# A token-mixer kernel: three small affine terms moved into weights, biases and spare rows, and a changed instruction order

## The chip, the cores and the metric

The kernel runs on one core of one Trainium2 chip. The metric is the device time of one execution in microseconds (us), measured on the chip. Executions of one kernel differ by about 1 to 2% (410.51 to 417.81 us in the first four of the kernel before), so every ratio below compares fast executions of two kernels taken in the same rounds, and differences under about 2 us are not read as effects. On one core there is no second die to compare with, so an execution counts as "slow" only where it is more than 1.5% above the fastest of its kernel. The record marks three executions of the kernel before so.

Engine names: PE is TensorE (matmuls), PEld its weight loads, DVE is VectorE, ACT is ScalarE, POOL is GpSimd, SP is the queue that issues most DMAs.

## The reference, cut to what matters

```python
# attention: 8 batches, 8 heads, 576 positions, 64 dims per head
kv  = einsum('bhsd,bhse->bhde', k, v)
out = einsum('bhsd,bhde->bhse', q, kv)
x   = out / sqrt(mean(out*out, -1) + 1e-6) * g_norm        # then heads side by side: (8, 576, 512)

# residual MLP: token mix, then channel mix
a1  = alpha1 * x + beta1
tok = einsum('ts,bsd->btd', w_tok, a1)                     # 576 x 576
u   = x + lam * tok
a2  = alpha2 * u + beta2
ch  = maximum(a2 @ w_ch1, 0) @ w_ch2                       # 512 -> 2048 -> 512
return u + lam * ch
```

Inputs and outputs are fp32. The kernel does the large products in bf16, and those of q, k and v at a higher precision: either in the fp32r type, or with a value split in two bf16 parts.

The affine terms beta1, alpha2 and beta2 can be moved without changing the result. With `d` for the channel and `t` for the token:

- beta1 contributes `rowsum(w_tok)[t] * (lam*beta1)[d]` to `u`. That is an outer product, so it can be extra K rows (rows that the matmul sums over) of the token-mix matmul.
- `a2 @ w_ch1 = u @ (diag(alpha2) w_ch1) + beta2 @ w_ch1`. The first factor is a scaled weight, the second a bias per hidden unit, which a ReLU instruction can add.

## The kernel before

The program is a list of operations with their dependencies, and a list scheduler in Python puts them in order on each engine before the kernel is built. Each operation has an estimated cost, one or several engines that may do it, and a priority; `hasten` gives everything that the first channel matmuls need the highest priority. So a change of any operation or of its estimated cost can change the order of all others.

"Channel 1" means the product with w_ch1 and the ReLU, "channel 2" the product with w_ch2. Batches are taken in pairs: an even batch has 512 columns, the odd one takes the 64 + 64 remaining tokens of both and has 640. The order is software-pipelined: while batch b is in its channel products, batch b+1 is normalised and token-mixed, and batch b+2 has its k, v and q prepared.

The parts that the argument touches:

```python
        def qkv_groups(b):
            def group(cs, hs):
                ...                                                   # q.kv on PE, mean square on ACT and DVE
                P.op("DVE", dve_us(64 * m), lambda e: e.tensor_tensor(                            # L621
                    out=x3, in0=raw(True), in1=inv(), op=ALU.mult), ...)
                P.op(dve_pool(64 * m) if b == 0 else "DVE", dve_us(64 * m),                       # L625
                     lambda e: e.tensor_tensor(out=r_, in0=x, in1=eb, op=ALU.mult), ...)
                P.op("POOL", pool_us(64 * m), lambda e: e.tensor_tensor(                          # L627
                    out=x3, in0=x3, in1=gb, op=ALU.mult), r=xk + ["g"], w=xk, pri=-50)
                if hs.stop == NH:
                    for c in cs:
                        ...
                        P.op("DVE", dve_us(560), lambda e, xa=xa, wc=wc:                          # L634
                             e.scalar_tensor_tensor(
                            out=xa, in0=e2_bc[rows, :], scalar=wsum[rows, wc:wc + 1], in1=xa,
                            op0=ALU.mult, op1=ALU.add), ...)
        ...
        def tok_out(b, c, t):
            ...
            P.op("DVE", dve_us(512), lambda e: e.tensor_tensor(                                   # L655
                out=x, in0=t.flat(rows), in1=x, op=ALU.add), r=[t] + xk, w=xk, pri=-100)
            if b == 0 and c < 4:
                return
            either = {"DVE": dve_us(512), "POOL": pool_us(512)} if b == 0 else "POOL"
            P.op(either, pool_us(512), lambda e: e.tensor_tensor(                                 # L660
                out=a1f[rows, af, :], in0=x, in1=a2_bc[rows, :], op=ALU.mult),
                r=xk + ["a2"], w=[("a1f", af)])
            P.op(either, pool_us(512), lambda e: e.tensor_tensor(                                 # L663
                out=a2b[rows, c, :], in0=a1f[rows, af, :], in1=b2_bc[rows, :],
                op=ALU.add), r=[("a1f", af), "b2"],
                w=[("a2b", c) if c < 4 else ("a2bt", b % 2)])
        ...
        def ut_groups(b):
            def group(c):
                keys = [("a2b", c)] if c < 4 else [("a2bt", 0), ("a2bt", 1)]
                if b > 1:                                             # else by PE
                    P.op("SP", 1.3, lambda e: e.dma_start_transpose(
                        a2t[:, :, 128 * c:128 * c + 128], a2b[:, c, :]), ...)
        ...
            def relu(t, src, dst, key, n):
                P.op("ACT", act_us(n), lambda e: e.activation(dst, src(), ACT.Relu),              # L769
                     r=[t], w=key)
        ...
        def load_w(i):
            if i < 4:
                ...                                                   # w_ch1, by DMA, to stg
                for dj in range(4):
                    P.op({"ACT": act_us(512), "POOL": 0.15 + 512 * 0.0016}, 0,
                         lambda e, dj=dj: copy(
                        e, w1[:, dj, 512 * i:512 * i + 512], stg[:, i % 3, dj]), ...)
            else:
                ...                                                   # w_ch2, by DMA, to stg
                for hh in range(4):
                    P.op(dve_pool(512), 0, lambda e, hh=hh: e.tensor_tensor(                      # L1046
                        out=w2[:, 4 * n + hh, :], in0=stg[:, i % 3, hh], in1=lam_bc[:],
                        op=ALU.mult), ...)
```

Cuts are marked with `...`; the line numbers were added and are those of the profile. `eb` is lam\*alpha1\*g_norm, `e2_bc` lam\*beta1, `wsum` the row sums of w_tok. Not shown: q of every batch is split in two bf16 parts (a cast, L415, and a subtraction, L473), and both are transposed to `qt`, by PE for the first batches and by DMA for the others. In the profile `a2b` is a block of a2 in bf16, `a2t` its transpose (what channel 1 reads), `ht` the output of the ReLU, `kr` and `vr` the rounded k and v, `qs` the split q, and `ps` a tile in PSUM.

## Time and profile before

Median of three executions: 412.77 us (410.51 to 416.17). The profiled execution, a fourth, took 417.36 us and has a span of 415.6 us (the time of an execution is about 1.8 us more than its span, in every run).

First, from the page of the kernel before: the busy line, the busy tenths of PE and DVE in 40 equal slices of the span, and the chain that ended last with its shares by engine and by line.

```profile
PE 378.7 (91%) x2584; PEld 221.5 (53%) x2297; DVE 277.6 (67%) x447; ACT 162.9 (39%) x302; POOL 190.6 (46%) x144
...
PE   7987876997799999999899999998999999959995
...
DVE  6349999999699766996896249897862269510011
...
PE 60%; DVE 27%; ACT 4%; DMA 4%; issue 3%; POOL 1%; POOLq 0%; SPq 0%; DVEq 0%
```

PE is the busiest engine, and the strip says where it has gaps: in the first eleven slices (114 us). DVE is at 9 from the fourth to the tenth of them (31 to 104 us). The chain says the same in another way: 27% of it, some 112 us, is DVE. POOL is busy 46% of the time and holds 1% of the chain.

The same in stretches, cut at the first channel-1 matmul of batch 0 (53.2), just after that of batch 1 (it starts at 114.4, the cut is at 114.6) and at the end of PE's work (411.1). Columns: stretch, its length, busy time and count of each engine, granted PE clock, DMA share, GB/s.

```profile
0.00:53.20 53.20, 45.11 (x279) 26.77 (x244) 36.89 (x72) 31.02 (x63) 26.13 (x29) 1.00 0.92 302
53.20:114.60 61.40, 49.30 (x390) 34.29 (x351) 57.57 (x75) 23.06 (x48) 39.97 (x25) 0.92 0.53 153
114.60:411.10 296.50, 284.28 (x1920) 160.40 (x1704) 182.48 (x301) 108.85 (x193) 124.52 (x90) 0.98 0.46 113
```

Between 53 and 115 us DVE is busy 57.6 of 61.4 us: that stage is DVE's. After that PE is busy 284 of 296.5 us: a stage that is PE's, with holes. (In the first stretch 14.0 us of PE's work are its 53 warm-up matmuls, which compute nothing.)

The groups of instructions that the change removes or touches (before, forms kept apart; columns: line, engine, operation, out<-in, shapes, count | busy us, mean ns of one | idle time before, and what ended it):

```profile
L769 ACT ACTIVATE ht<-ps 128x640 bf16<-128x640 f32 x64 | 44.9, 702 | 46.5 <-PE ps L793 46.3
...
L663 POOL TENSOR_TENSOR a2b<-a1f,b_bc 128x512 bf16<-128x512 f32 x28 | 39.8, 1420 | 2.2
...
L660 POOL TENSOR_TENSOR a1f<-xm,a_bc 128x512 f32<-128x512 f32 x28 | 38.8, 1386 | 15.2 <-DVE xm L655 13.6
L634 DVE SCALAR_TENSOR_TENSOR xm<-e_bc,wsum,xm 128x512 f32<-128x512 f32 x32 | 30.4, 956 | 0.3 <-POOL xm L627 0.2
L473 DVE TENSOR_TENSOR qs<-qf,qs 128x512 bf16<-128x512 f32 x30 | 29.7, 1014 | 4.0 <-ACT qs L415 3.7
```

With their half-height forms, L660 and L663 are 101.0 us of POOL and L634 is 38.6 us of DVE.

Last, the largest hole of the third stage, in the chain in order of time (start us, length us, what), around the last channel 1:

```profile
357.87 6.92 PE ps L841 x32
...
364.81 0.70 DVE xm L850
...
365.52 1.28 POOL a2b L663
...
366.87 1.26 POOL a1f L660
...
368.17 1.31 POOLq L345
...
369.50 3.82 DMA a2t<-a2b
...
373.37 20.46 PE ps L793 x128
```

Here PE's last channel 1 cannot start because POOL is still in its alpha2 and beta2 passes and a DMA transpose must follow them. The 128 matmuls after the hole take 20.46 us. The hole costs its own 5.1 us of waiting and, by the estimate below, about 2.9 us more. These lie where the trace shows a halved clock: the granted clock is 0.50 from 372.5 to 379.3, and the matmuls in that time start every 267 ns, against 136 later in the same row, at 1.00. At 136 ns each the 5.9 us of matmuls in that time would have taken about 3.0 (an estimate from the two spacings). So at this hole 5.1 us of idle PE go with 5.9 us of matmuls at 0.50.

### The profile page before, as it was taken

The page shows a single profiled execution, that of the slowest core. Times are in us where ns is not written, and L with a number is a line of the kernel's source. Part 1 is how long each engine was busy: PE and PEld are TensorE (multiplying, and loading weights), DVE is VectorE, ACT ScalarE, POOL GpSimd, SP SyncE. Part 2 cuts the span into 40 slices and gives each one's busy share as a digit, 9 for nine tenths or more (in the row PEclk, how much of TensorE's full clock was granted, in tenths as well). Part 3 has the DMA queues.
Part 4 walks back from the last instruction along what each step waited for, and adds up shares of the span by engine and source line. Part 5 has one row for each costly group of instructions (what it writes and reads, how often), then busy time and mean ns, then how long its engine had stood idle before and what let it go on. Part 6 is the DMA issues. An engine that isn't in the chain of part 4 may idle for free.

```text
span 415.6 us, 6149 instructions
## 1 busy us (share of the span) xinstructions
PE 378.7 (91%) x2584; PEld 221.5 (53%) x2297; DVE 277.6 (67%) x447; ACT 162.9 (39%) x302; POOL 190.6 (46%) x144
## 2 busy tenths in 40 slices
PE   7987876997799999999899999998999999959995
PEld 3664475843577445545575455445764554426642
DVE  6349999999699766996896249897862269510011
ACT  3569363800288024910483018502740065004600
POOL 5318568459214880469046902494449015650000
PEclk9999998999699999999899999999999999997998
DMA  8997886207797939917974319715413210140012
GB/s 250 373 352 256 267 288 197 98 0 177 187 316 81 202 105 274 224 46 201 200 184 126 101 59 265 134 35 115 91 27 78 77 27 1 50 115 0 2 50 76
DMA packets 95737, 59.29 MB, mean 143 GB/s; under 512 B 61847, under 2 KB 86423, under 8 KB 95708
## 3 DMA queue, kind: packets, MB, share of 16 engines
q1 hardware_dynamic: 94640, 58.88, 52.3%
q8 instruction: 19, 0.31, 0.3%
q10 hardware_dynamic: 1068, 0.01, 0.2%
q14 instruction: 10, 0.08, 0.1%
HBM read 38.04 MB, written 9.44 MB: 114 GB/s over the span
## 4 chain that ended last, share of the span: by engine, by line
PE 60%; DVE 27%; ACT 4%; DMA 4%; issue 3%; POOL 1%; POOLq 0%; SPq 0%; DVEq 0%
PE ps L841 21%; PE ps L793 16%; PE ps L778 7%; PE ps L678 4%; PE ps L508 4%; DVE xm L634 4%; DVE qs L473 4%; DVE rt L625 3%; PE ps L899 2%; DVE xm L655 2%; DVE kr L416 2%; DMA qf<-in_q_dram 2%; DVE w L1046 2%; DVE xm L621 2%; PE ps L572 1%
## 5 line engine op out<-in xcount | busy, mean ns | idle before, releaser
L841 PE MATMUL ps<-w,ht 128*128 128x512 bf16 x556 | 127.3, 380 | 1.6 <-DVE xm L850 0.3
L769 ACT ACTIVATE ht<-ps 128x640 bf16<-128x640 f32 (+2 forms) x104 | 78.6, 760 | 61.2 <-PE ps L793 46.3
L627 POOL TENSOR_TENSOR xm<-xm,g_bc 128x512 f32<-128x512 f32 x32 | 44.4, 1389 | 114.8 <-DVE rt L625 114.5
L841 PEld LDWEIGHTS ps<-w,ht 128*128 128x128 bf16 x576 | 55.4, 98 | 65.1 <-DVE xm L850 1.0
L793 PE MATMUL ps<-a2t,w 128*128 128x320 bf16 x512 | 76.6, 311 | 5.1 <-DMA a2t<-a2b 5.1
L850 DVE TENSOR_TENSOR xm<-ps,xm 128x512 f32<-128x512 f32 x32 | 22.0, 690 | 68.9 <-PE ps L841 68.6
L793 PEld LDWEIGHTS ps<-a2t,w 128*128 128x128 bf16 x512 | 50.9, 101 | 27.0 <-DMA a2t<-a2b 5.6
L663 POOL TENSOR_TENSOR a2b<-a1f,b_bc 128x512 bf16<-128x512 f32 (+1 forms) x36 | 53.0, 1472 | 10.0 <-DVE a1f L660 7.2
L524 ACT ACTIVATE kvd<-ps 64x128 bf16<-64x128 f32 x32 | 8.7, 271 | 101.8 <-PE ps L508 101.6
L660 POOL TENSOR_TENSOR a1f<-xm,a_bc 128x512 f32<-128x512 f32 x28 | 38.8, 1386 | 15.2 <-DVE xm L655 13.6
L778 PE MATMUL ps<-a2t,w 128*128 128x512 bf16 x185 | 43.2, 379 | 0.4
L678 PE MATMUL ps<-rt,wt 128*128 128x512 bf16 x173 | 39.2, 379 | 2.1 <-DVE xm L655 1.4
L508 PE MATMUL ps<-vr,kr 128*128 128x256 f32 x160 | 27.8, 324 | 6.0 <-DVE a2t L416 3.9
L473 DVE TENSOR_TENSOR qs<-qf,qs 128x512 bf16<-128x512 f32 x30 | 29.7, 1014 | 4.0 <-ACT qs L415 3.7
L599 DVE TENSOR_REDUCE small<-sq 128x8 f32<-128x512 f32 (+2 forms) x41 | 26.5, 660 | 7.9 <-ACT sq L597 7.8
L634 DVE SCALAR_TENSOR_TENSOR xm<-e_bc,wsum,xm 128x512 f32<-128x512 f32 x32 | 30.4, 956 | 0.3 <-POOL xm L627 0.2
L572 PE MATMUL ps<-kvd,qt 128*128 128x64 bf16 x320 | 23.7, 195 | 7.4 <-DVE kvd L532 7.4
L678 PEld LDWEIGHTS ps<-rt,wt 128*128 128x128 bf16 x175 | 16.7, 98 | 23.6 <-DVE xm L655 3.2
L572 PEld LDWEIGHTS ps<-kvd,qt 128*128 128x128 bf16 x320 | 21.5, 99 | 13.7 <-DVE kvd L532 8.7
L508 PEld LDWEIGHTS ps<-vr,kr 128*128 128x128 f32 x160 | 24.1, 215 | 8.7 <-DVE a2t L416 4.4
L778 PEld LDWEIGHTS ps<-a2t,w 128*128 128x128 bf16 x192 | 17.8, 98 | 19.8 <-DMA a2t<-a2b 0.5
L597 ACT ACTIVATE sq<-ps 128x512 f32<-128x512 f32 (+2 forms) x41 | 23.1, 580 | 9.7 <-PE ps L322 9.4
(93 smaller groups left out, 423.2 us busy)
## 6 DMA issues: line engine op xcount, KB each, us to landing
qf<-in_q_dram SPq DMA_DIRECT2D x8, 1024.0 KB, 6.7
stg<-in_moe_w_ch_dram SPq DMA_DIRECT2D x8, 1024.0 KB, 8.8
out_dram<-xm SPq DMA_DIRECT2D x32, 256.0 KB, 3.0
kf<-in_k_dram SPq DMA_DIRECT2D x7, 1024.0 KB, 5.2
vf<-in_v_dram SPq DMA_DIRECT2D x7, 1024.0 KB, 7.3
qft<-in_q_dram SPq DMA_DIRECT2D x8, 128.0 KB, 5.5
kf<-in_k_dram SPq DMA_DIRECT2D x2, 512.0 KB, 6.2
kft<-in_k_dram SPq DMA_DIRECT2D x8, 128.0 KB, 6.4
```

The costliest lines, as they stand in the source:

```text
L473: P.op(dve_pool(512) if b == 0 else "DVE", dve_us(512), lambda e, hi=hi, lo=lo, src=src: e.tensor_tensor(out=lo, in0=src, in1=hi, op=ALU.s ...
L508: m = e.matmul(o, flat(kr[:, c, 2 * pr:2 * pr + 2, :]), flat(vr[:, c, 4 * a:4 * a + 4, :]), start=(c == 0), stop=(c == 4))
L572: e.matmul(o, w, kvd[:, h, 0, :], start=True, stop=False)
L627: P.op("POOL", pool_us(64 * m), lambda e: e.tensor_tensor(out=x3, in0=x3, in1=gb, op=ALU.mult), r=xk + ["g"], w=xk, pri=-50)
L634: e.scalar_tensor_tensor(out=xa, in0=e2_bc[rows, :], scalar=wsum[rows, wc:wc + 1], in1=xa, op0=ALU.mult, op1=ALU.add),
L660: P.op(either, pool_us(512), lambda e: e.tensor_tensor(out=a1f[rows, af, :], in0=x, in1=a2_bc[rows, :], op=ALU.mult), r=xk + ["a2"], w=[(" ...
L663: P.op(either, pool_us(512), lambda e: e.tensor_tensor(out=a2b[rows, c, :], in0=a1f[rows, af, :], in1=b2_bc[rows, :], op=ALU.add), r=[("a1 ...
L678: m = e.matmul(t.flat(), wt[:, ws, tok_col(b, c):tok_col(b, c) + 128], rt[:, sc, :], start=(sc == 0), stop=(sc == 4))
L769: P.op("ACT", act_us(n), lambda e: e.activation(dst, src(), ACT.Relu), r=[t], w=key)
L778: m = e.matmul(t.ap()[:, i, :], w1[:, dj, 128 * (fj + i):128 * (fj + i) + 128], a2t[:, dj, 0:512], start=(dj == 0), stop=(dj == 3))
L793: m = e.matmul(t.ap()[:, i, 0:320], w1[:, dj, 128 * fj:128 * fj + 128], a2t[:, dj, 320 * i:320 * i + 320], start=(dj == 0), stop=(dj == 3))
L841: m = e.matmul(t.flat(), ht[:, fj, 128 * c:128 * c + 128], w2[:, fj, :], start=(fj == 0), stop=(fj == 15))
```

## The change

The intent, in five parts:

1. **alpha2 into w_ch1, beta2 into the ReLU bias.** w_ch1 is scaled by alpha2 while it is cast; beta2 @ w_ch1 is computed by 64 small matmuls, which need a second, unscaled bf16 copy of w_ch1. The two POOL passes of every block become one cast.
2. **beta1 into spare K rows of the token mix.** The last K chunk holds 64 tokens in 128 rows. Four of the empty rows get lam*beta1 and the row sums of w_tok, each in two bf16 parts. The DVE pass L634 goes.
3. **q.kv of the first batch in fp32r**, so that its q needs no split.
4. **A changed scheduler.** PE takes work first that has been ready for 1 us; operations of POOL and the marked ones of DVE (`lock`; the q subtractions and the k and v casts are among them) are planned one after the other, never side by side; an engine may be held idle for hastened work that is about to be ready. The ReLUs of batch 0's channel 1 now count as hastened too.
5. Smaller: weight casts of w_tok in bf16 on POOL, row sums on PE, the fourth part of w_ch1 loaded to a place of its own, and the ReLUs of batch 0's channel 1 shared by ACT and DVE. The ReLUs of the even batches also cover half as many columns each (512 and 256 instead of 1024 and 512), and some small buffers have more copies.

The diff, cut to its core (cuts marked with `...`):

```diff
-                        P.op("DVE", dve_us(560), lambda e, xa=xa, wc=wc:
-                             e.scalar_tensor_tensor(
-                            out=xa, in0=e2_bc[rows, :], scalar=wsum[rows, wc:wc + 1], in1=xa,
-                            op0=ALU.mult, op1=ALU.add),
-                            r=ka + ["e2", "wsum"], w=ka, pri=60)
...
-            P.op(either, pool_us(512), lambda e: e.tensor_tensor(
-                out=a1f[rows, af, :], in0=x, in1=a2_bc[rows, :], op=ALU.mult),
-                r=xk + ["a2"], w=[("a1f", af)])
-            P.op(either, pool_us(512), lambda e: e.tensor_tensor(
-                out=a2b[rows, c, :], in0=a1f[rows, af, :], in1=b2_bc[rows, :],
-                op=ALU.add), r=[("a1f", af), "b2"],
-                w=[("a2b", c) if c < 4 else ("a2bt", b % 2)])
+            P.op({"ACT": act_us(512), "POOL": 0.15 + 512 * 0.0011}, 0, lambda e: copy(
+                e, a2b[rows, c, :], x), r=xk, w=[("a2b", c) if c < 4 else ("a2bt", b % 2)],
+                pri=-100)
...
+                    if e is nc.scalar:
+                        return e.activation(dst, src(), ACT.Relu, bias=cb[:, fj:fj + 1])
...
-                         lambda e, dj=dj: copy(
-                        e, w1[:, dj, 512 * i:512 * i + 512], stg[:, i % 3, dj]),
+                    P.op({"ACT": act_us(512), "POOL": 0.75}, 0, lambda e, dj=dj: scaled(
+                        e, w1[:, dj, 512 * i:512 * i + 512], st[:, dj],
+                        ab2[:, 0, dj:dj + 1]),
...
+                    P.op({"ACT": act_us(512), "POOL": 0.75}, 0, lambda e, dj=dj: copy(
+                        e, w1u[:, dj], st[:, dj]), r=[sk], w=[("w1u", i % 2, dj)], pri=40)
...
+                            m = e.matmul(t.flat()[:, 2 * fj:2 * fj + 2],
+                                         w1u[:, dj, 128 * fj:128 * fj + 128], b2h[:, :, dj],
+                                         start=(dj == 0), stop=(dj == 3))
...
+                    if e == "PE" and not first:
+                        cands = ([o for o in cands if ready(o, t - self.margin)]
+                                 + [o for o in cands if not ready(o, t - self.margin)])
...
-            if o not in targets and o.eng != "SP":
+            if o.eng != "SP":
                 o.pri = -1000.0 - way
...
+                        if held(o, e, t):
+                            continue
...
-        split_q(0)
-        qt_dma(0)
+        qt_first()
```

## The prediction

> **What bounds the kernel now.** TensorE, with holes. The page has PE busy 378.7 of 415.6 us, DVE 277.6, POOL 190.6, ACT 162.9. In the chain of waits PE holds 60% and DVE 27%, and the DVE pieces lie almost all in the first 110 us. Three stages, by the timelines:
> - 0 to 53.2 us: up to the first channel matmul (L808). PE only fills in with warm-up matmuls (L1098, 53 of them). The DVE chain normalise, e1g product (L625), beta1 term (L634), token add (L655) sets the end.
> - 53 to 114.6 us: DVE is 98% busy (windows 40 to 100 us). Channel 1 of batch 0 needs 13.8 us of PE but its last stretch ends at 81.8, and batch 1's channel 1 starts only at 114.6. Here L473 takes 1.3 to 1.7 us, against 0.67 unhindered, while POOL runs a1f/a2b/g products.
> - 114.6 us to PE's end at 411.1: 296.5 us. With 16 128x512 matmuls in 3.45 us (chain of waits), the remaining matmuls need about 278 us. The rest is holes: about 1 us at 180 and 267, 2.2 us at 198 and 285 and 5.5 us at 364.8, where PE waits for POOL's a1f, a2b and the DMA transpose, plus slow matmuls after each (the last 128 L793 took 20.5 us instead of 17.4).
>
> **What the change does, costed.**
> - beta1 into spare K rows: 40 L634 on DVE go (38.6 us in all, about 4.8 us a batch); the wsum work goes.
> - alpha2/beta2 folded: L660 and L663 go (101 us of POOL). One copy per block is left, which the built order puts on ACT (about 0.62 us). Tail of token mix to a2b falls from about 2.8 us a block to 0.6. Less POOL means less waiting of DVE [...]; the 0.67 against 1.67 us of L473 agrees.
> - fp32r q.kv for batch 0: drops the hi/lo split of q (5 casts, 5 subtractions, of these 5.6 us on POOL) and the kvd correction.
> - Added: second bf16 copy of w_ch1 (16 casts of 0.6 to 0.96 us on ACT/POOL), 64 two-column matmuls, ReLUs with bias halved (ACT about +2.5 us per even batch). ACT becomes the limit of the start beside DVE: 19 weight casts, about 12 us, precede its a2t copies.
> - Order: channel 1 of batch 0 runs as one block of 128 matmuls with ReLUs shared by ACT and DVE; the fourth w_ch1 load no longer waits for staging. Channel 2 of the last odd pair leaves 52 matmuls (11 us) to hide the last a2b/a2t.
>
> **Estimate.**
> - First channel matmul at about 49 us, the block ends at about 63. Then DVE must round k/v, split q and copy q^T for batch 1 before channel 2 starts: about 76. Batch 1's channel 1 at about 101, so 13 us saved up to there.
> - Later holes: of 18 us, about 14 go.
> - Together about 27 us: span about 388, timed median 386 us (412.8 before), range 376 to 397.
>
> **What would show it.** DVE busy near 230 us, POOL near 95, ACT near 190 to 200. L1098 fewer than 53. Batch 1's first 128x320 matmul near 101 us. From there to PE's end 280 to 284 us, with no hole over 1.5 us and no wait for a2t by DMA. L473 (L522 now) near 0.75 us.
>
> **What would make it wrong.** ACT's in-order queue of weight casts delaying a2t (first channel matmul after 55 us); kv(1)/q split after batch 0's channel 1 leaving PE idle over 15 us; TensorE's new preference for long-ready work delaying token mix and opening holes in steady state; or better overlap at 62 to 100 us than I allow (then about 375).

## The result, and the profile after

The changed kernel took 392.37 us (median of four, 389.41 to 393.35): faster, by 5.1%. The ratio is 0.9485, 95% interval 0.9382 to 0.9588. (A ratio here is the mean time of one kernel's fast executions over that of the other's of the same rounds, so it is not quite the ratio of the medians quoted.) It was run again beside the experiments as a control, c_after: 391.32 us, ratio 0.9448 (0.9372 to 0.9525).

The page of the kernel after, the same lines as before:

```profile
PE 363.7 (93%) x2566; PEld 217.5 (56%) x2319; DVE 237.2 (61%) x423; ACT 196.2 (50%) x365; POOL 98.3 (25%) x80
...
PE   4988995599989999899999999999999999999995
...
DVE  5498659999879448791897138954853248410021
...
PE 82%; DVE 7%; DMA 5%; ACT 3%; issue 1%; ACTq 0%
```

POOL lost 92 us of work, DVE 40, and ACT gained 33. The chain is now 82% PE and 7% DVE. In the strip PE is at 8 or 9 from the second slice to the last but one, except for one dent that is new: the two slices at 5, which are 58.7 to 78.3 us.

In stretches, cut at the first and the last channel-1 matmul of batch 0 (43.5, 57.7), at the first channel-2 matmul (78.4), at batch 1's channel 1 (102.6) and at the end of PE's work (387.0):

```profile
0.00:43.50 43.50, 34.14 (x247) 23.09 (x252) 30.16 (x68) 28.92 (x60) 25.14 (x31) 0.92 0.99 294
43.50:57.70 14.20, 14.14 (x128) 12.61 (x129) 8.15 (x19) 11.03 (x23) 10.95 (x10) 1.00 0.96 303
57.70:78.40 20.70, 12.40 (x144) 10.91 (x105) 19.22 (x27) 8.56 (x18) 11.52 (x6) 0.78 0.56 169
78.40:102.60 24.20, 23.34 (x127) 12.27 (x129) 23.56 (x39) 8.91 (x19) 7.92 (x5) 0.97 0.49 110
102.60:387.00 284.40, 279.71 (x1921) 158.58 (x1706) 155.41 (x274) 138.74 (x247) 42.73 (x30) 1.00 0.53 126
```

Side by side, from the two traces (us from the start of the span):

| | before | after | saved by then |
|---|---|---|---|
| first channel-1 matmul, batch 0 | 53.2 | 43.5 | 9.7 |
| last one of batch 0 | 81.8 | 57.7 | 24.1 |
| first channel-2 matmul, batch 0 | 81.8 | 78.4 | 3.4 |
| first channel-1 matmul, batch 1 | 114.4 | 102.6 | 11.8 |
| end of PE's work | 411.1 | 387.0 | 24.1 |

So the lead is 9.7 us at the first channel matmul and 24.1 at the end of batch 0's channel 1, which now runs as one block of 14.1 us (before, its two halves lay around other work, 28.6 us from first to last). But that other work has only been put behind the block: by the first channel-2 matmul, 20.7 us later, the lead is down to 3.4. It is 11.8 at batch 1's channel 1, and the long PE-bound rest brings the other 12.3 (296.7 to 284.4 us). Some 3 of these 24.1 us belong to the traced executions and not to the change: the trace of before is of an execution of 417.36 us, where the mean of its fast ones in those rounds is 413.15; the ratio makes the whole gain 21.3 us.

What PE waits for in the new dent is in the chain in order of time (after; start us, length us, what):

```profile
43.52 14.14 PE ps L898 x128
57.71 1.04 PE ps L769 x4
58.78 0.68 DVE xtl L751
59.46 1.13 DVE kr L465
60.59 1.13 DVE vr L465
61.73 6.75 DVE qs L522 x4
68.51 1.65 DVE qs L522
...
78.42 10.08 PE ps L935 x43
```

Batch 1's k had landed at 41.8 us (issued at 34.5, 7.3 us on the way), but DVE rounds it (kr) only at 59.5, and then v (vr), and splits q (qs) after that, in four steps of 1.7 us each and one of 1.65. Then PE itself is slow: from 72.9 to 79.7 the granted clock is 0.50, and the small q.kv matmuls of batch 1 start every 53 ns instead of every 29 (as they do after 100 us in the same trace, at 1.00), so that they take 4.5 us, about 2 us more than at the full clock (an estimate from the two spacings). During the block before, 43.5 to 57.7, DVE was busy just 8.2 of 14.2 us. So PE is short of work here because DVE prepares batch 1 now, and not sooner, though it had the time; in the order that the scheduler made, the hastened ReLUs of batch 0 come first.

At the other end the large hole is gone. The same chain, around the last channel 1:

```profile
344.41 7.93 PE ps L935 x36
352.34 17.39 PE ps L882 x128
```

And the groups (after; the forms that answer to those shown of before). The alpha2 and beta2 passes are now one ACT cast of 0.63 us, and L634 has no successor:

```profile
L859 ACT ACTIVATE ht<-ps,cb 128x640 bf16<-128x640 f32 x64 | 50.5, 796 | 26.7 <-PE ps L882 26.0
...
L522 DVE TENSOR_TENSOR qs<-qf,qs 128x512 bf16<-128x512 f32 x28 | 28.4, 1059 | 3.8 <-ACT qs L464 3.6
...
L464 ACT ACTIVATE a2b<-xm 128x512 bf16<-128x512 f32 x28 | 17.5, 630 | 28.1 <-DVE xm L751 28.0
```

### The profile page after: what moved, and what is told of

Same layout as the page of the kernel before. It is cut to its first block, busy times and chain, and to the rows that moved or that the text cites. A ratio compares the mean times of both kernels' runs of the same rounds, so it can differ in the third digit from the quotient of the medians.

```text
span 391.5 us, 6123 instructions
## 1 busy us (share of the span) xinstructions
PE 363.7 (93%) x2566; PEld 217.5 (56%) x2319; DVE 237.2 (61%) x423; ACT 196.2 (50%) x365; POOL 98.3 (25%) x80
## 4 chain that ended last, share of the span: by engine, by line
PE 82%; DVE 7%; DMA 5%; ACT 3%; issue 1%; ACTq 0%
PE ps L935 31%; PE ps L882 14%; PE ps L769 11%; PE ps L869 9%; DMA qt<-qs 4%; PE ps L586 4%; PE ps L898 4%; DVE qs L522 2%; PE ps L678 2%; PE ps L359 2%; PE ps L1264 1%; DMA xtl<-in_g_norm_dram 1%; ACT ht L859 1%; PE ps L998 1%; PE ps L555 1%
## 5 line engine op out<-in xcount | busy, mean ns | idle before, releaser
L859 ACT ACTIVATE ht<-ps,cb 128x640 bf16<-128x640 f32 (+2 forms) x129 | 90.7, 713 | 36.8 <-PE ps L882 26.0
L736 POOL TENSOR_TENSOR xm<-xm,g_bc 128x512 f32<-128x512 f32 x28 | 39.2, 1400 | 210.1 <-DVE rt L732 209.9
L882 PE MATMUL ps<-a2t,w 128*128 128x320 bf16 x512 | 73.2, 300 | 2.9 <-ACT ht L859 2.2
L944 DVE TENSOR_TENSOR xm<-ps,xm 128x512 f32<-128x512 f32 x32 | 22.0, 690 | 76.2 <-PE ps L935 76.1
L882 PEld LDWEIGHTS ps<-a2t,w 128*128 128x128 bf16 x512 | 48.5, 98 | 24.0 <-ACT ht L859 3.8
L769 PE MATMUL ps<-rt,wt 128*128 128x512 bf16 x185 | 43.4, 391 | 1.5 <-DVE wt L1020 1.2
L769 PEld LDWEIGHTS ps<-rt,wt 128*128 128x128 bf16 x190 | 18.9, 100 | 24.0 <-issue 2.2
L464 ACT ACTIVATE a2b<-xm 128x512 bf16<-128x512 f32 x28 | 17.5, 630 | 28.1 <-DVE xm L751 28.0
L522 DVE TENSOR_TENSOR qs<-qf,qs 128x512 bf16<-128x512 f32 x28 | 28.4, 1059 | 3.8 <-ACT qs L464 3.6
L751 DVE TENSOR_TENSOR xm<-ps,xm 128x512 f32<-128x512 f32 x32 | 21.5, 689 | 14.2 <-PE ps L769 12.9
L869 PEld LDWEIGHTS ps<-a2t,w 128*128 128x128 bf16 x192 | 17.9, 98 | 20.9 <-ACT ht L859 1.1
L586 PE MATMUL ps<-vr,kr 128*128 128x256 f32 x160 | 25.4, 308 | 3.0 <-DVE vr L465 3.0
L464 ACT ACTIVATE qs<-qf 128x512 bf16<-128x512 f32 x28 | 16.9, 627 | 10.8 <-DMA qf<-in_q_dram 5.7
```

The costliest lines, as they stand in the source:

```text
L464: return e.activation(out, in_, ACT.Identity)
L522: P.op("DVE", dve_us(512), lambda e, hi=hi, lo=lo, src=src: e.tensor_tensor(out=lo, in0=src, in1=hi, op=ALU.subtract), r=kin + [kh], w=[kl ...
L586: m = e.matmul(o, flat(kr[:, c, 2 * pr:2 * pr + 2, :]), flat(vr[:, c, 4 * a:4 * a + 4, :]), start=(c == 0), stop=(c == 4))
L736: lambda e: e.tensor_tensor(out=x3, in0=x3, in1=gb, op=ALU.mult),
L769: m = e.matmul(t.flat(), wt[:, ws, tok_col(b, c):tok_col(b, c) + 128], rt[:, ws, :], start=(sc == 0), stop=(sc == 4))
L859: return e.activation(dst, src(), ACT.Relu, bias=cb[:, fj:fj + 1])
```

## The experiments

The question after the result was which part of the change had brought the time, and why the dent at 58 to 78 us is there. Twelve kernels were run, in four groups; within a group all ran on one chip, beside the kernel before. All are changes of the kernel after. The control c_after ran in the first group only, so a difference from it in us is one between chips; the medians of the kernel before in the four groups, 414.2 to 415.4 us, say how little that adds.

| run | what is different from after | us, median | ratio to before (95%) | ch 1 batch 1 starts | rest to PE's end |
|---|---|---|---|---|---|
| c_after | nothing | 391.32 | 0.9448 (0.9372 to 0.9525) | 100.6 | 286.3 |
| e3_old_scheduler | scheduler as before | 389.80 | 0.9406 (0.9320 to 0.9492) | 98.0 | 286.5 |
| e6_bf16_first | first batch's q split again | 389.68 | 0.9383 (0.9314 to 0.9451) | 100.7 | 280.9 |
| e9_relu_no_bias | ReLU without the bias operand | 390.22 | 0.9430 (0.9383 to 0.9477) | 100.2 | 282.8 |
| e4_beta1_on_dve | a beta1 pass on DVE, all reordered | 404.41 | 0.9778 (0.9697 to 0.9859) | 107.6 | 293.7 |
| e4f_beta1_same_order | the same, order of the rest kept | 400.94 | 0.9695 (0.9618 to 0.9771) | 107.7 | 287.7 |
| e5_a2_on_pool | two POOL passes, all reordered | 419.42 | 1.0134 (1.0063 to 1.0205) | 129.2 | 283.4 |
| e5f_a2_same_order | the same, order of the rest kept | 402.75 | 0.9723 (0.9680 to 0.9767) | 109.5 | 285.5 |
| e13_a2_full_operand | as e5f, with full-size operands | 412.67 | 1.0011 (0.9930 to 1.0093) | 112.4 | 291.6 |
| e12_both_same_order | e4f and e13 together | 431.13 | 1.0382 (1.0326 to 1.0439) | 118.8 | 305.1 |
| e7m_w2_memset_on_pool | POOL writes a constant for w2 | 389.25 | 0.9397 (0.9357 to 0.9437) | 98.2 | 284.0 |
| e10_hold_qtlat | holding ends with channel 1; one latency | 386.98 | 0.9331 (0.9268 to 0.9393) | 98.6 | 280.2 |

The last two columns come from the one profiled execution of each kernel, in us. Profiled executions of one kernel differ too (after and c_after have 284.4 and 286.3 in the last column), so 2 us there mean nothing.

### c_after: the control

The changed kernel itself, run with the first group.

> The changed kernel again, as the control of this set. All theories: 389 to 394 us, batch 1's first 128x320 channel matmul at about 102.5 us, PE idle between 57.7 and 78.4 us except for about 7 us.

It took 391.32 us, against 392.37 at first. Batch 1's channel 1 started at 100.6 us, and between batch 0's channel 1 and channel 2 (58.5 to 76.2) PE was busy for 11.0 us, not 7. What follows is compared with these two.

### e3_old_scheduler: the order rules undone

```diff
-        self.patience = 0.15
-        self.margin = 1.0
+        self.patience = 1e9
+        self.margin = 0.0
...
-            if o.eng != "SP":
+            if o not in targets and o.eng != "SP":
...
-            return e == "POOL" or (e == "DVE" and o.lock)
+            return False
```

> The changed kernel's operations under the old list scheduler: no preference for long-ready work on TensorE, no holding back for urgent work, [...] the last channel-1 group of batch 0 not hastened. Theory A: the operations made the gain, the scheduler shapes only the first 100 us: 2 to 8 us slower than the control, first channel matmul later than 43.5 us. Rival C (the order made most of the gain): 12 us or more slower, near the time before.

A miss. It took 389.80 us, which can't be told from the control. The way there differs: channel 1 of batch 0 starts 2.7 us later (47.3 against 44.6) and is again split, until 75.3, but channel 2 starts as that ends (75.1) and batch 1's channel 1 at 98.0. The one tight block of channel 1 that the new rules make is paid back in full by the dent after it. The four rules of the scheduler, taken together, are worth nothing here. (One of them is the last of the diff, which plans POOL's operations and the marked ones of DVE apart.)

### e6_bf16_first: the first batch's q split again

```diff
-        P.op("DVE", 0.8, lambda e: e.memset(kvb[:].bitcast(F32), 0.0), w=["kvb0"])
-        qt_first()
+        split_q(0)
+        qt_dma(0)
```

(and the q.kv of batch 0 by the path of the other batches)

> The changed kernel with batch 0's q.kv as before: q split in a high and a low bf16 half by ACT, DVE and POOL, transposed, multiplied with split kv; the order is made anew. Theory: 5 casts, 5 subtractions and the kv corrections return to ACT and DVE before 30 us: first channel matmul 2 to 4 us later, the same 2 to 4 us at the end. Rival (the start is set by the weight casts on ACT, not by q.kv): within 1 us.

It took 389.68 us: no slower. The first channel matmul is at 45.3 us, against 44.6 in the control. So what the fp32r product saves at the start was not on the path that sets the start, and this part of the change is worth nothing measurable either.

### e9_relu_no_bias: what the bias operand costs

```diff
-                        return e.activation(dst, src(), ACT.Relu, bias=cb[:, fj:fj + 1])
+                        return e.activation(dst, src(), ACT.Relu)
```

This drops beta2 from ACT's ReLUs; beta2 is so small that the result stays within the tolerance.

> The changed kernel with the ReLUs on ACT without their bias operand (a wrong result on purpose); same order on every engine. In the traces the 640-column ReLU takes 796 ns with the bias against 702 before, the 512-column one 686. If the bias operand is what costs it: 702 and 596 ns again, ACT busy down by about 11 us to 185. Theory: ACT is not the limit after 102 us, so the time moves by less than 3 us. Rival: the holes that end on a ReLU (2.9 us before 128x320 matmuls) shrink and 4 us or more are won.

The groups of ReLUs in this run (all forms of L859):

```profile
L859 ACT ACTIVATE ht<-ps 128x640 bf16<-128x640 f32 x64 | 44.5, 702 | 30.3 <-PE ps L882 30.1
L859 ACT ACTIVATE ht<-ps 128x512 bf16<-128x512 f32 x48 | 28.1, 597 | 9.3 <-PE ps L869 8.5
```

The 640-column ReLU takes 702 ns without the bias and 796 with it, the 512-column one 597 against 686: 89 to 94 ns for the operand, at either size. ACT is 10 us less busy here (186.2 against 196.2 to 196.5), and the time is 390.22: 1 to 2 us less, as the theory had it. ACT at 50% has room for it.

### e4_beta1_on_dve and e4f_beta1_same_order: what beta1 is worth

A DVE pass of the same form as L634 is put back on every block. It adds zero times an operand, so the result stays right.

```diff
+                if hs.stop == NH:
+                    for c in cs:
+                        xa, ka = xv(b, c), xkeys(b, c)
+                        P.op("DVE", dve_us(560), lambda e, xa=xa: e.scalar_tensor_tensor(
+                            out=xa, in0=e1g_bc[rows, :], scalar=zc[rows, :], in1=xa,
+                            op0=ALU.mult, op1=ALU.add), r=ka + ["e1", "zc"], w=ka, pri=60)
```

> The changed kernel with a DVE pass over each normalised block put back (plus e1g times a zero column), as the beta1 term was; result unchanged. Theory A: DVE busy rises by about 38 us to 275, but steady state has room for it; it costs 1 to 3 us in the start (about 5 passes before token mix of batch 0 and of batch 1) and 0 to 4 us later, in all 1 to 7 us. Rival B (DVE's load is the main cause): 8 us or more.

It took 404.41 us, 13 more than the control: past Theory A's 1 to 7 and, at face value, Rival B. But the scheduler knew of the added passes and reordered everything, so this mixes the pass with a new order. Hence the second version: the pass goes in as an operation that costs the scheduler nothing, takes no turn on an engine, and is bound to DVE when the order is final. The order of all other instructions is that of the kernel after.

```diff
-                        P.op("DVE", dve_us(560), ...)
+                        P.op("GHOST", 0.0, ...).real = "DVE"        # placed, at no cost, where it is ready
```

> The 40 DVE passes of the beta1 term put back, but inserted into the changed kernel's order after it was made: every engine's order is the changed kernel's, with 41 DVE instructions more and nothing else moved. It splits the 13 us that putting them back had cost. Theory D (most of those 13 us came from the order the list scheduler then found, not from the DVE work): 3 to 6 us slower than the changed kernel, most of it before 110 us. Rival B (DVE's work is itself on the path in steady state too): 10 us or more, with PE's time after batch 1's first channel matmul at 292 us or more.

It took 400.94 us, 9.6 more than the control. The added passes take 34.7 us of DVE (905 ns for a full one), which is near the 38.6 of L634. The loss lies early: the first channel matmul is at 49.6 (control 44.6) and batch 1's channel 1 at 107.7 (100.6). From there to the end of PE's work it is 287.7 us, within 2 us of the control. So beta1 is worth about 10 us, nearly all of it before batch 1's channel 1, where DVE is the limit in the last stretch (in this run it is busy 28.07 of the 28.75 us from 78.9 to 107.65, in the kernel after 23.56 of 24.2); what went of it later saved nothing that these runs can measure. Neither expectation was right as a whole: the cost is close to Rival B's in size (10 or more), but it lies where Theory D put it, before 110 us.

### e5_a2_on_pool and e5f_a2_same_order: what the alpha2/beta2 fold is worth, first try

Two POOL passes are put back between the token add and the bf16 block, with operands of one column (1 and 0), so the result is right. The weights stay scaled and the ReLUs keep their bias.

```diff
-            P.op({"ACT": act_us(512), "POOL": 0.15 + 512 * 0.0011}, 0, lambda e: copy(
-                e, a2b[rows, c, :], x), ...)
+            P.op(either, pool_us(512), lambda e: e.tensor_tensor(
+                out=a1f[rows, :], in0=x, in1=oz[rows, 0:1].to_broadcast(...), op=ALU.mult), ...)
+            P.op(either, pool_us(512), lambda e: e.tensor_tensor(
+                out=a2b[rows, c, :], in0=a1f[rows, :], in1=oz[rows, 1:2].to_broadcast(...),
+                op=ALU.add), ...)
```

> The changed kernel with the one ACT copy per block replaced by two POOL passes over the block (times one, plus zero), as alpha2/beta2 were before; weights, ReLU bias and result unchanged. Theory A (POOL's latency before the transposes made the steady-state holes; this is the largest part of the gain after 102 us): POOL busy rises by about 100 us to about 200, PE waits for a2t again before the last channel 1 and at the odd batches, PE's time from batch 1's first channel matmul to its end goes from 284.5 to 294 us or more; in all 8 to 14 us slower than the control. Rival B (DVE's load was what mattered, POOL is off the path): within 3 us of the control.

It took 419.42 us, more than the kernel before. The time is lost after channel 2 of batch 0 has started (79.7): PE then stands still for 4.6, 2.3, 2.3, 6.4 and 5.4 us until batch 1's channel 1 at 129.2. By the list of waits the 6.4 us end with POOL's second pass and the others with work of DVE, which here has its q split and its copies ahead of what PE waits for. The rest takes 283.4 us, no more than in the control, so Theory A's later holes did not come. As a price of the two passes this run is of no use, so they were put in again without reordering:

> The one ACT copy per block replaced by two POOL passes, in the changed kernel's order (36 ACT copies out, 72 POOL passes in, nothing else moved). With the order made anew it cost 28 us, all of it between 77 and 129 us. Theory D (the new order was the cost): 6 to 14 us slower than the changed kernel, with holes of 3 to 8 us before the last channel 1 and at every odd batch's a2t. Theory A' (the POOL chain itself costs it at batch 1, where POOL still scales w_ch2 and multiplies by g): 20 us or more, over 15 of it before batch 1's first channel matmul.

It took 402.75 us, 11.4 more than the control, within Theory D's range, but without its late holes. So of the 28 us of e5 some 17 were the order. Again it is all early: batch 1's channel 1 starts at 109.5 (100.6), the rest takes 285.5 us. But these passes are too cheap. POOL took 1.05 to 1.08 us for one with a one-column operand, while L660 and L663 of the kernel before took 1.39 and 1.42 (means; the medians are 1.04 us for the one-column pass and 1.27 for the other two), and the late holes of the kernel before did not come back. A pass of another length can't say what the original was worth; so there is a third version.

### e13_a2_full_operand: the same with operands of full size

```diff
-                out=a1f[rows, :], in0=x, in1=oz[rows, 0:1].to_broadcast(...), op=ALU.mult)
+                out=a1f[rows, :], in0=x, in1=e1g_bc[rows, :], op=ALU.mult)
...
-                out=a2b[rows, c, :], in0=a1f[rows, :], in1=oz[rows, 1:2].to_broadcast(...), op=ALU.add)
+                out=a2b[rows, c, :], in0=a1f[rows, :], in1=lam_bc[rows, :], op=ALU.add)
```

The operands are any two tiles at hand, so the values are wrong (the result still fell within the tolerance, as the channel term is multiplied by a small lam).

> The two POOL passes for every block alone, in the changed kernel's order, now with the full 512-wide second operand (a wrong result on purpose, inside the tolerance): the missing corner of the two-by-two. With the one-column operand (1.10 us a pass) this cost 11 us, none of it after batch 1's first channel matmul; with beta1's DVE passes back as well (and the full operand, 1.33 us a pass) it cost 40 us, 20 of them after that point. Theory E (the DVE passes and the POOL passes make the later holes only together): 402 to 407 us, PE's time after batch 1's first channel matmul under 290 us. Rival G (the longer POOL passes alone make them): 412 us or more, that time 295 us or more.

It took 412.67 us, 21.3 more than the control: nearly all of the gain is gone with this one part undone. A full pass takes 1.28 to 1.30 us on the mean, a little less than L660 and L663 took, and 1.27 on the median, as they did. The total is Rival G's (412 or more), its rest of 295 us is not reached. In this run's chain, one sees both places where it hurts. First, before batch 1's channel 1 (start us, length us, what):

```profile
90.40 1.28 POOL half L768
...
91.75 1.27 POOL a2b L771
...
93.09 2.13 POOL xm L749
...
103.48 1.60 POOL a2b L771
...
105.22 0.38 PE ps L859 x4
```

For 15 us the chain is POOL alone: four blocks, two passes each, with two g products between. Batch 1's channel 1 starts at 112.4 instead of 100.6. Second, in the PE-bound rest, where the two passes end in a DMA transpose that PE waits for:

```profile
197.30 1.30 POOL half L768
...
198.66 1.28 POOL a2b L771
199.96 2.43 DMA a2t<-a2b
...
202.43 2.35 PE ps L899 x16
```

In the list of PE's waits of this run, channel 1 of the odd batches waited for such a transpose three times, 3.2 us in all; the kernel after has no such wait. The rest takes 291.6 us (284.4 and 286.3 in the two traces of the kernel after). So the fold is worth about 21 us: about 12 of them early, in POOL's chain ahead of batch 1, and about 5 to 7 later. (The profiled execution, 410.22 us, was 2.5 us shorter than the median, so the split is rougher than the sum.)

### e12_both_same_order: both undone

The edits of e4f and e13 together.

> Both undone at once in the changed kernel's order: the 40 DVE passes of beta1 and, for every ACT copy of a block, two POOL passes with a full 512-wide second operand as before (the earlier undo had a one-column operand, 1.10 us a pass against 1.40 in the kernel before); a wrong result on purpose. Alone in this order the first cost 9 to 10 us (2 of it after batch 1's first channel matmul), the second 11 us (none after it), so 12 us that the change won after that point are not explained yet. Theory E (they are won by removing both: the two chains follow one another in each batch, and the holes appear only when both are there): PE's time after batch 1's first channel matmul goes to 293 us or more, total 412 us or more. Rival F (those 12 us come from something else in the change: one-bank ReLU groups, more small buffers): it stays under 289 us, total 405 to 411.

It took 431.13 us, with a rest of 305.1 us: as Theory E had it, and not Rival F. In the order of the kernel after, one has a full square:

| | no beta1 pass | beta1 pass |
|---|---|---|
| **no POOL passes** | 391.3 | 400.9 (+9.6) |
| **POOL passes** | 412.7 (+21.3) | 431.1 (+39.8) |

Together they cost 8.9 us more than the sum of each (by the ratios, 0.0934 against 0.0247 + 0.0563, times 414 us, it is 5, and from the four intervals I estimate an uncertainty of about 6). So the times alone don't establish that it is more than a plain sum. The traces point to it, one execution each: the rest after batch 1's first channel 1 grows by 18.8 us over the control's, against 1.4 and 5.3 for each alone, and PE's channel 1 waits for the DMA transposes 9.9 us in all, against 3.2 in e13. DVE's extra pass lies ahead of POOL's two on the way to the same transpose, so that a delay of each ends in the same wait; that this is why the rest grows by more than the sum is my reading of the chain, not a test.

That both undone are 16 us slower than the kernel before needs a word. The kernel after adds work (16 more weight casts, a bias on every ReLU), and its order was made for a kernel without these passes; the kernel before had an order made for them. I take that as the reason. It was not tested, beyond what e4 against e4f and e5 against e5f show: that the order alone moves the time by 3.5 and by 17 us.

### e7m_w2_memset_on_pool: why the q split is slow in the dent

In the dent DVE's four q subtractions took 6.75 us, 1.75 to 1.78 each, while POOL was scaling w_ch2 by lam (L1211); with no POOL product beside them others of the same trace took 0.67 to 0.69. The intended test, of whether it is POOL's reading that slows them: let POOL write a constant in place of the product. (So the result is wrong, with a relative error of 6.6.)

```diff
-                    P.op(dve_pool(512), 0, lambda e, hh=hh: e.tensor_tensor(
+                    P.op(dve_pool(512), 0, lambda e, hh=hh: e.memset(
+                        w2[:, 4 * n + hh, :], 0.01) if e is nc.gpsimd else e.tensor_tensor(
```

> The 13 scalings of w_ch2 on POOL (21.5 us from 48 to 70 us) made constant writes that read nothing (a wrong result on purpose); same order on every engine. Theory: [...] batch 1's q subtractions take 1.7 us each; without them 0.69 us, kv and the q transposes follow 4 to 6 us earlier, channel 2 of batch 0 starts at 72 to 74 us instead of 76 to 78.4, and 3 to 6 us are left at the end. Rival (the subtractions are slow for another reason, or the time there is set by ACT's copies of q^T): channel 2 starts within 1.5 us of the changed kernel's.

The q split between 40 and 80 us in the kernel after, and POOL's work on w_ch2 (duration ns: min, median, max; first and last start us; shape):

```profile
L522 DVE TENSOR_TENSOR qs<-qf,qs x4: 1748/1760/1777, 61.7 to 66.7; 128x512 bf16<-128x512 f32 x4
...
L1211 POOL TENSOR_TENSOR w<-stg,lam_bc x13: 1264/1273/3977, 48.1 to 68.0; 128x512 bf16<-128x512 f32 x13
```

And the same views of this run:

```profile
L522 DVE TENSOR_TENSOR qs<-qf,qs x4: 676/676/678, 62.2 to 64.0; 128x512 bf16<-128x512 f32 x4
...
L1211 POOL MEMSET w<- x13: 525/525/526, 47.6 to 57.9; 128x512 bf16 x13
```

The same instruction at the same time takes 0.68 us instead of 1.76, and channel 2 starts at 73.3 us (76.2 and 78.4 in the two traces of the kernel after). So it was POOL's scaling beside it that made it slow. But the run doesn't test reads against writes: a constant write takes 0.53 us and a product 1.27 or more, so the writes were over by 58.5 us, and POOL stood idle when the q split began at 62.2. That a write alone would not slow DVE is not shown, beyond one small sign: in the trace of the kernel before a DVE product of one partition, 1x512, runs half its time beside a POOL memset (4.67 to 5.35 us, the memset until 5.02) and takes 0.68 us, and two more like it, with POOL idle, take 0.68 and 0.67. In c_after just two of the five subtractions were slow (1.76 us), and channel 2 started at 76.2 us. The whole kernel took 389.25 us, only 2 to 3 us less, at the edge of what is read here as an effect: the dent has other parts, and even without the contention it lasts 15.4 us (57.9 to 73.3).

### e10_hold_qtlat: the dent taken away

The rule that holds an engine for hastened work is switched off as soon as the first channel matmul has started, so that DVE may prepare batch 1 between its ReLUs. And the scheduler is told a longer latency for the DMA transposes of q (2.5 us; the trace shows 3.19, 5.63 and 7.56 us in the chain, the old figure was 0.8).

```diff
         def held(o, e, t):
+            if self.warm[0].start is not None:
+                return False
...
-                        dma_us=0.8)
+                        dma_us=2.5)
```

> A try to beat the changed kernel, two edits of its list scheduler alone. First: other work is held back for urgent work only until the first channel matmul is placed, so that DVE rounds k and v and splits q of batch 1 in the gaps between batch 0's ReLUs (43 to 58 us) rather than after them. Second: the DMA transposes of q are planned with 2.5 us each instead of 0.8 (the traces show 3 us), so that ACT's casts of the next q, which wait for them, are queued behind more ReLUs. Theory: channel 2 of batch 0 starts at 68 to 72 us instead of 76 to 78.4, the two ReLU holes of 1.3 to 1.5 us at 109 and 161 us go; 6 to 10 us faster, 381 to 386 us. Rival: POOL's scaling of w_ch2 holds up DVE there just the same and batch 0's block stretches: within 2 us.

It took 386.98 us (385.11 to 388.19), 4 to 5 us less than the kernel after (389.15 to 393.35 in its eight executions; the ranges don't touch, but these ran on other chips, and the intervals of the ratios overlap a little: up to 0.9393 here, from 0.9372 in c_after). Its median is the lowest of all; e6, on the same chip, took 387.33 to 391.48. So it is probably, not certainly, faster than the kernel after. The gain is less than I had expected, and channel 2 starts at 74.1 us, not at the 68 to 72 of my expectation. In the trace the q split of batch 1 now lies within the channel-1 block (51 to 57 us), still slowed in part by POOL (same view as above, this run):

```profile
L525 DVE TENSOR_TENSOR qs<-qf,qs x4: 726/1358/1755, 51.1 to 55.1; 128x512 bf16<-128x512 f32 x4
```

What then follows is a wait for ACT's ReLUs (L862, until 62.6), since DVE does fewer of them: 25 of 32 are ACT's, against 17 in the kernel after. In the rest, PE waits no more for ACT's ReLUs in the middle of a channel 1 (3.3 us in the kernel after, where ACT stood behind a q cast that waited for a transpose). Which of the two edits brings how much was not separated.

## Why the prediction was right or wrong, point by point

**Right: the class and the range.** 386 us, 376 to 397, was predicted, 392.4 was measured: faster, and inside the range.

**Right: which costs go.** DVE is at 237 us (predicted near 230), POOL 98 (near 95), ACT 196 (190 to 200). The tail of a block from token mix to bf16 is 0.63 us, as predicted (0.6). Warm-up matmuls are 18, fewer than 53. PE has no wait for a2t by DMA, and the hole at 364.8 us is gone.

**Right in direction, 2 us off in size: the PE-bound rest.** "280 to 284 us" was 284.4. "Of 18 us, about 14 go": 12.3 went. "No hole over 1.5 us" held narrowly: the longest is 1.48 us, at 109.6, where PE waits for a ReLU because ACT stood behind a q cast.

**Wrong, and hidden by a second error: the first 103 us.** "First channel matmul at about 49 us" was 43.5: I had added up ACT's queue of weight casts as if it were the limit, and it was not. "The block ends at about 63 [...] channel 2 starts: about 76" then meant 13 us between the two, and 20.7 were measured (57.7 to 78.4). The mis-sized term is the q split, "L473 (L522 now) near 0.75 us": in that gap it took 1.65 to 1.78 us, five times, with POOL's w_ch2 scaling beside it. That is 4.9 us more than five times 0.75, of the 7.7, and the halved clock of the q.kv matmuls, which I had not foreseen, is about 2 more (an estimate from their spacing, above). In c_after, with two slow subtractions, the gap was 17.7 us; in e7m, with none, 15.4, still over my 13. I had reasoned that less POOL means less contention. On the average that did not show: the mean of this line over the whole kernel was 1014 ns before, 1059 after and 969 in c_after. In the trace of after the eleven subtractions over 1.6 us all had a POOL product beside them for about two thirds of their time or more (w_ch2 scaling or a g product), and those with none took 0.67 to 0.69. But six with a g product beside them for three quarters of their time or more took 0.68 to 0.69 as well. So it isn't the amount of POOL's work that goes with the slow ones but its falling beside the DVE instruction, which still happens, and not each time that it does; what else decides was not shown. The two errors, a start 5.5 us too late and a gap 7.7 us too short, nearly cancel, which is why "batch 1's channel 1 at about 101" looks right (102.6). My own warning, "leaving PE idle over 15 us", came true in kind but not in size: PE was idle for 8.3 of the 20.7 us.

**Wrong by 3 us: from span to time.** The profiled span after is 391.5, against a predicted 388; I then took off 2 us because the median of before was 2.8 us under its profiled span. That offset is chance: an execution takes about 1.8 us more than its span, and the profiled one of before, at 417.36 us, was just a long one. After has a median 0.9 us above its span. Of the error of 6.4 us, 3.5 are thus in the span and about 3 in this step.

**Not foreseen: the bias operand.** I costed the ReLUs by their number alone. Each also pays about 90 ns for the bias, 10 us of ACT in all (e9). It cost at most the 1 to 2 us of e9, since ACT isn't the limit.

**Not separated in the prediction, and shown by the runs: where the gain comes from.** I had put the three causes side by side. Undone one at a time, the alpha2/beta2 fold is worth 21 us, beta1 10, the fp32r product and the scheduler nothing that these runs can measure. And the fold's gain isn't found where POOL's busy time is: POOL held 1% of the chain before. It is POOL's place that made it dear, two passes in a row between DVE's token add and the transpose that channel 1 needs (by PE for batch 1, by DMA later). Conversely, of the 38.6 us of DVE work that beta1 cost, only the part ahead of batch 1's channel 1 was worth anything that could be measured.

**Open.** Why the start is at 43.5 rather than 49 is told by the trace only in part (ACT's casts ended at 41.1, and ACT then sat idle for 1.5 us until PE's transposes came, so it was not the last to arrive). Which edit of e10 gives its gain, and how the half-clock stretch in the dent could be avoided, was not tried. Part 5 of the change, with the smaller ReLUs and the larger buffers, was not undone on its own either, so a share of it in the gain is not excluded.

## What to carry to other kernels

An affine term on the way from one matmul to the next is worth more than its share of busy time if it sits on a slow engine between a producer and a transfer that TensorE waits for (here POOL, at 1.27 us on the median for a pass of 128x512, had 1% of the chain, and the fold of its two passes was worth 21 us): look for the chain "engine pass, engine pass, DMA, matmul" rather than for the busiest engine, and fold such a term into a weight or a bias first. When the order comes from a scheduler, price a part by undoing it with the order of all else kept, and with operands of the same size; both mattered here by more than the effect (17 us between two orders, 10 us between a one-column and a full operand). And when a two-input DVE operation is slow, as the q subtraction was here (up to 1.78 us, against 0.68 with POOL idle), ask whether POOL runs a two-input operation at that moment, not how busy POOL is over the whole kernel.

## What the traces show of the clock, of POOL and of the DMA transposes

Four things measured here that may be of use elsewhere:

- The granted clock after a gap in PE's work. It was 0.50 after the gap of 5.1 us above (372.5 to 379.3), and after shorter ones too: 1.98 us in the kernel before (198.7 to 200.7; 0.50 from 201.8 to 205.2) and 1.2 us in the kernel after (34.0 to 35.2; 0.50 from 35.3 to 38.7). After another gap of 1.96 us in the kernel before (at 286) and one of 1.48 us in the kernel after (at 108.1) the clock stayed full. What decides between them, these runs don't show.
- POOL's times for 128x512. A two-input `tensor_tensor` with an operand of full size took 1.27 us on the median (before); with the second operand broadcast from one column it was quicker, 1.04 us on the median (e5f). A scaled weight cast, `tensor_scalar` with a per-partition operand, took 1.56 to 2.54 us, 2.10 on the mean, while a plain cast took 0.66 and the same scaled cast on ACT 0.71 (kernel after). The kernel's own scheduler counts 0.75 us for it.
- DVE beside POOL. A 128x512 DVE subtraction took 1.75 to 1.78 us where it alternated with POOL's products (after), and 0.68 us with POOL idle (e7m).
- The DMA transpose of a 128x512 bf16 block, which feeds channel 1: 2.43 us in e13 and 3.82 us in the kernel before, each as it stands in the chain of waits.
